# Low words of the last tile of probabilities written straight into their rows by VectorE, and the places of all heads' steps chosen anew

## The chip, the core and the metric

The kernel runs on one core of a Trainium2 chip. The core has five engines that work side by side and wait for each other by semaphores: TensorE (PE in the profile; its weight loads are PEld), VectorE (DVE), ScalarE (ACT), GpSimd (POOL), and SyncE (SP), which here only issues DMAs. Each engine runs its own instructions strictly in the order in which the program has them. The metric is the device time of one launch in microseconds. It is compared as the median of several runs.

## The reference

Attention over 8 batches of 8 heads (576 tokens, 64 columns a head) with a decay and a causal mask, then a mixer that works along the tokens and along the channels:

```python
decay = cum[:, :, :, None] - cum[:, :, None, :]
scores = np.where(causal, -1000000000.0, scale * q @ k.T + decay)
attn = np.exp(scores - max); attn = attn / (sum + 1e-09)
x = (attn @ v) laid out as [8, 576, 512]
u = x + (relu(x.T @ w_tok1) @ w_tok2).T     # w_tok1 576x256, w_tok2 256x576
out = u + relu(u @ w_ch1) @ w_ch2            # w_ch1 512x1536, w_ch2 1536x512
```

The first two lines are shortened. The weights come as float64 and are taken apart to float32 on the chip ("decoded").

## The kernel before, in words

**Precision.** PE multiplies float32 in a rounded form (fp32r in the profile). A product that must be exact is made of three: an operand is split into its high word, which is the rounded value, and its low word, which is the value minus the high word. High times high, high times low and low times high are summed in PSUM. "Low word" in what follows is always such a difference, written by a subtract (`lo_dve`, line 593, on DVE; `lo_pool`, line 590, on POOL).

**One head**, in the order of its data:
- POOL splits q and k of two heads (line 818 the high words, 826 the low ones); SP gathers them by DMA into k1 and k2 (line 873), and the decay rows into k2 (line 867).
- PE makes the scores (line 900), five tiles of rows, in PSUM. DVE adds the mask and takes the minimum (line 907, followed by a short read of the accumulator, nmin). ACT takes the exponential with the sum of each row (line 914).
- DVE makes the reciprocals (lines 932 and 935); POOL multiplies the rows by them (line 942).
- PE transposes the probabilities into PSUM (line 956) in four groups: tiles 3 and 4, tile 2, tile 1, and tile 0, which has only 64 rows of keys. For each group ACT writes the high words (line 584) and DVE the low words (line 593), into p34, p2 and p1 with both words beside each other.
- Tile 0 goes into p0, a buffer of 128 partitions: high words in partitions 0 to 63, low words in 64 to 127, so that one product with 128 rows serves both. Before the change DVE writes the low words into a buffer of their own, `low` (64 partitions, 576 columns, two subtracts of 64 and 512 columns), and POOL moves the 576 columns into the lower half of p0 (line 587). The first product with V (lines 1026 and 1027) waits for that move.
- PE multiplies with V (lines 1026 to 1038); ACT and DVE add the halves into xt (lines 1076, 1083, 1086).

Heads 0 to 3 take a short way without low words, so that the move stands in the program 60 times.

**The mixer** of a batch (transposes of xt in line 1576; the two products along the tokens in 1609 to 1612 and 1633 to 1635; the first two of twelve column blocks of the channel products in 1678 to 1680 and 1706 to 1708) is laid between the heads of the next batch, since PE would wait there. Its weights are decoded tile by tile, eight steps each on ACT, DVE and POOL (lines 682 to 702 and the split behind them), between the first 16 heads or so. The rest of the channel weights comes in 20 units of 512 columns; the first two are taken through lines 682 to 702 early, behind heads 15 to 17. After the last head the attention's buffers are given up, the other units are decoded into the space (on DVE above all), and PE makes the other ten column blocks: 768 tokens in plain form (lines 1219 to 1241), the rest with seven instead of eight products of blocks (lines 1365 to 1367 and 1440 to 1442).

**What sets the order.** The program does not write its order out. `build` gives every operation an engine, an estimated duration, a priority, and what it reads, writes and holds; `Plan.run` then plays all five engines forward, always giving a free engine the operation with the least priority number that can start by the estimates, and the sequence that comes out is the program. The priority is the head's number plus an offset of the kind of step (OFF), one of the head's place in its batch (STEP), and one of the head itself (HEAD, eight batches of eight heads). MIX, MIXB and DEC do the same for the mixer's pieces and the decode steps. In the kernel before, the HEAD and MIXB rows of batches 1 to 5 are zero: every batch there has the same places. POOL and those operations of DVE that are marked `port` are played so that one excludes the other, before the change only from batch 6 (PORT) on; earlier decode steps have longer durations instead.

Of the kernel before, what the change touches and what calls it, by code (L numbers as in the profile page):

```python
# [22 lines left out]
OFF = dict(
    load=-14.57, kh=71.94, kl=74.34, qh=-209.6, ql=-43.06, vh=-98.02, vl=123.3, s4=3.88, s3=5.49, s2=-16.37, mn=13.65,
    ex=8.87, rec=-4.02, nrm=-189.8, t3=3.09, t2=-115.31, t1=-82.69, t0=-39.76, hl=-31.61, av=-7.13, fold=-31.54,
    fpe=3.69, lo0=-44.75, fev=-192.41, u=-110.56, dec=70.59, dec2=33.11, dec3=78.27, cd=-12.6, vload=-16.33,
# [3 lines left out]
    cd=(-5.6, 64.49, 4.17, 0.29, 2.76, -5.41, -22.94, 0.01),  # L30
    kh=(17.78, -2.69, -14.75, 26.31, -2.51, -6.4, 0.84, -42.85),
    kl=(0.0, -0.21, -36.59, 1.3, -31.34, -30.51, -4.86, -5.93),
    s4=(21.98, 22.01, 19.66, -0.06, 3.68, 0.01, 62.36, 65.83),
    s3=(-5.96, 1.74, -17.12, 5.63, -13.9, 21.15, 0.16, -24.96),
    s2=(-9.31, 12.57, -3.01, -10.47, -58.87, 1.25, -0.3, -9.41),
    mn=(-20.45, -3.64, -9.81, -2.84, 19.06, -18.82, 40.74, -47.15),
    ex=(-8.49, -16.56, -25.97, 0.0, -26.61, 6.71, -17.69, 0.28),
    rec=(11.69, -16.14, -0.04, 23.14, 14.55, -4.69, 14.63, 10.44),
    nrm=(-1.09, -0.04, 34.13, -18.17, 0.0, -5.71, -23.45, -1.03),
    t3=(-47.4, -43.09, 1.3, -15.85, 0.37, -0.2, 4.51, 4.91),  # L40
    t2=(2.19, -5.45, 0.3, -22.18, 0.0, 0.51, -38.74, 2.55),
    t1=(0.03, -7.68, 5.88, 3.1, -4.1, 0.72, 10.85, 9.62),
    t0=(-29.97, 31.91, -0.46, -7.92, -108.28, -1.02, -12.55, -3.15),
    hl=(36.2, -1.08, -2.52, 2.48, 30.49, 0.0, 30.12, -19.09),
    av=(165.0, -24.98, -1.39, 1.47, -1.66, -6.57, -8.96, -9.8),
    fold=(0.54, -18.69, -70.99, 0.85, -5.32, -1.54, 57.67, -26.27),
    load=(2.05, 29.47, -1.17, -17.23, 19.8, -6.84, 2.87, 9.6),
    vload=(-5.04, 0.0, 12.21, 13.64, -0.05, 6.27, 6.41, 34.92),
    qh=(0.7, 8.11, 0.0, 0.33, 17.69, -21.0, -0.25, -0.16),
    lo0=(-2.15, 2.18, 0.0, 8.97, 0.04, -0.79, 0.22, -8.44),  # L50
# [6 lines left out]
    cd=(  # L57
# [8 lines left out]
    ),  # L66
    kh=(
# [475 lines left out]
def build(nc, env, dims):  # L543
# [20 lines left out]
    def d_act(n, ps=True, ptr=0):  # L564
        return 0.833 * n + (51 if ps else 93) + 93 * ptr + (130 if n > 512 else 0)
# [1402 lines left out]
```

## Time and profile before

| | us |
|---|---|
| median of 3 runs | 1083.37 (1082.1 to 1083.46) |
| the profiled execution | 1080.26 |
| its span | 1078.4 |
| DMA k<-hl on the chain that ended last | 6.5% of the span |
| HBM traffic over the span | 178 GB/s |

The profile shows one execution. A row of the groups view names the line of the kernel, the engine, the operation, the buffer written and those read (numbers left out), their shapes and the count; then the busy time in us, the mean of one in ns, and how long the engine idled just before these instructions, with what ended the idling. The waits view sums the same idling by who waited for whom. The windows view cuts the span into stretches. PE's clock was granted in full nearly throughout (0.995 on average). Times in rows of the timeline count from the start of the span.

### The profile page before, as it was taken

The page shows a single profiled execution, that of the slowest core. Times are in us where ns is not written, and L with a number is a line of the kernel's source. Part 1 is how long each engine was busy: PE and PEld are TensorE (multiplying, and loading weights), DVE is VectorE, ACT ScalarE, POOL GpSimd, SP SyncE. Part 2 cuts the span into 40 slices and gives each one's busy share as a digit, 9 for nine tenths or more (in the row PEclk, how much of TensorE's full clock was granted, in tenths as well). Part 3 has the DMA queues.
Part 4 walks back from the last instruction along what each step waited for, and adds up shares of the span by engine and source line. Part 5 has one row for each costly group of instructions (what it writes and reads, how often), then busy time and mean ns, then how long its engine had stood idle before and what let it go on. Part 6 is the DMA issues. An engine that isn't in the chain of part 4 may idle for free.

```text
span 1078.4 us, 20528 instructions
## 1 busy us (share of the span) xinstructions
PE 1028.6 (95%) x6442; PEld 914.1 (85%) x6442; DVE 886.8 (82%) x2117; ACT 646.8 (60%) x1607; POOL 496.8 (46%) x579
## 2 busy tenths in 40 slices
PE   8887989999999999999999899999999999999998
PEld 5566878899999999899998888877888888888887
DVE  7779989788887888878779999975995995797586
ACT  4776876788888888888777534522631541362142
POOL 4686897787868878688672100022311001102000
PEclk9999999999999999999999999999999999999999
DMA  8786785878768787686765699889899789879874
GB/s 207 187 205 144 189 211 142 205 194 201 206 174 214 198 204 204 160 221 184 216 183 188 219 328 320 260 278 346 300 304 354 237 261 342 285 218 344 247 202 148
DMA packets 143548, 248.71 MB, mean 231 GB/s; under 512 B 20760, under 2 KB 70680, under 8 KB 142416
## 3 DMA queue, kind: packets, MB, share of 16 engines
q1 hardware_dynamic: 143312, 247.39, 79.4%
q8 instruction: 52, 0.85, 0.3%
q14 instruction: 56, 0.46, 0.1%
q10 hardware_dynamic: 128, 0.01, 0.0%
HBM read 145.24 MB, written 46.66 MB: 178 GB/s over the span
## 4 chain that ended last, share of the span: by engine, by line
PE 68%; DMA 11%; DVE 10%; SPq 3%; POOL 3%; ACT 2%; issue 2%; DVEq 0%; POOLq 0%; ACTq 0%
DMA k<-hl 7%; PE bank L956 6%; PE bank L1365 5%; PE bank L1367 5%; PE bank L1366 5%; PE bank L900 4%; PE bank L1441 3%; PE bank L1440 3%; PE bank L1442 3%; PE pair L1441 2%; PE pair L1440 2%; PE pair L1442 2%; PE pair L900 2%; PE pair L1038 2%; PE pair L1036 2%
## 5 line engine op out<-in xcount | busy, mean ns | idle before, releaser
L942 POOL TENSOR_SCALAR pr<-pr,rec 128x576 f32<-128x576 f32 (+4 forms) x320 | 173.1, 561 | 37.2 <-DVE rec L935 29.5
L584 ACT ACTIVATE p<-bank 128x384 fp32r<-128x384 f32 (+2 forms) x300 | 128.1, 474 | 38.2 <-PE bank L956 36.3
L956 PE MATMUL bank<-ident,pr 128*128 128x128 f32 (+1 forms) x960 | 137.4, 276 | 7.9 <-DVE p L593 3.6
L914 ACT ACTIVATE pr<-bank,nmin 128x448 f32<-128x448 f32 (+3 forms) x256 | 118.2, 469 | 20.1 <-DVE nmin L907 17.8
L593 DVE TENSOR_TENSOR p<-bank,p 128x384 fp32r<-128x384 f32 (+1 forms) x180 | 105.9, 594 | 26.0 <-ACT p L584 25.0
L956 PEld LDWEIGHTS bank<-ident,pr 128*128 128x128 f32 (+1 forms) x960 | 107.9, 132 | 18.6 <-POOL pr L942 4.4
L907 DVE CUSTOM_DVE_ANT_0 bank<-bank,mask 64x64 f32<-64x64 f32 (+3 forms) x256 | 106.7, 432 | 14.3 <-PE bank L900 12.6
L900 PE MATMUL bank<-k 128*128 128x320 f32 (+1 forms) x496 | 87.3, 297 | 12.6 <-DMA k<-hl 7.7
L900 PEld LDWEIGHTS bank<-k 128*128 128x128 f32 x496 | 73.7, 175 | 25.7 <-DMA k<-hl 5.8
L826 POOL TENSOR_TENSOR hl<-raw,hl 128x1152 fp32r<-128x1152 f32 x28 | 74.8, 2670 | 1.4
L584 ACT ACTIVATE hid<-h 128x480 fp32r<-128x480 f32 x77 | 46.5, 605 | 48.2 <-PE bank L1441 27.0
L1038 PE MATMUL pair<-p,vv 128*128 128x512 f32 x240 | 74.0, 316 | 0.0
L1036 PE MATMUL pair<-p,vv 128*64 128x512 f32 x240 | 70.6, 335 | 0.0
L587 POOL TENSOR_SCALAR p<-low 64x576 fp32r<-64x576 f32 x60 | 42.1, 702 | 56.9 <-DVE low L593 48.5
L584 ACT ACTIVATE ring<-bank 128x288 fp32r<-128x288 f32 (+2 forms) x96 | 46.6, 496 | 20.4 <-PE bank L1576 7.3
L826 POOL TENSOR_TENSOR vv<-vr,vv 128x640 fp32r<-128x640 f32 x30 | 47.9, 1598 | 18.0 <-ACT vv L816 17.8
L593 DVE TENSOR_TENSOR low<-bank,p 64x64 fp32r<-64x64 f32 (+1 forms) x120 | 50.7, 441 | 6.6 <-ACT p L584 6.1
L1386 ACT ACTIVATE h<-bank 128x480 f32<-128x480 f32 x20 | 11.5, 573 | 73.5 <-PE bank L1367 73.5
L1377 ACT ACTIVATE tmp<-bank 128x480 f32<-128x480 f32 x20 | 11.4, 571 | 70.7 <-PE bank L1367 62.8
L590 POOL TENSOR_TENSOR ring<-xt,ring 128x576 fp32r<-128x576 f32 x32 | 45.1, 1421 | 18.5 <-ACT ring L584 17.9
L907 DVE CUSTOM_DVE_ANT_0 pair<-pair,mask 128x576 f32<-128x576 f32 x64 | 48.8, 762 | 5.8 <-PE pair L900 4.9
L584 ACT ACTIVATE st<-h 128x480 fp32r<-128x480 f32 x63 | 37.7, 604 | 25.7 <-PE bank L1441 9.4
(321 smaller groups left out, 3461.4 us busy)
## 6 DMA issues: line engine op xcount, KB each, us to landing
pw<-wd SPq DMA_DIRECT2D x280, 256.0 KB
k<-hl SPq DMA_DIRECT2D x186, 288.0 KB
raw<-in_qk SPq DMA_DIRECT2D x31, 576.0 KB
vr<-in_v SPq DMA_DIRECT2D x32, 320.0 KB
d_raw<-in_w_ch SPq DMA_DIRECT2D x80, 128.0 KB
ud<-xt SPq DMA_DIRECT2D x8, 1152.0 KB
pd<-part SPq DMA_DIRECT2D x32, 288.0 KB
wd<-pw SPq DMA_DIRECT2D x20, 384.0 KB
```

The costliest lines, as they stand in the source:

```text
L584: nc.scalar.activation(out, in_, func, scale=scale)
L593: nc.vector.tensor_tensor(out, in_, asf(hi), op=ALU.subtract)
L826: (nc.gpsimd if eng == "POOL" else nc.vector).tensor_tensor(out, in_, asf(hi), op=ALU.subtract)
L900: nc.tensor.matmul(ps[:m, of : of + w], k[:, 0, i0 : i0 + m], k[:, 1, j0 : j0 + w], start=(x == 0), stop=(fq or x == 1))
L907: nc.vector.tensor_tensor_reduce(x, x, E["mask"][:m, a : a + w], -1.0 / D**0.5, 3e38, op0=ALU.add, op1=ALU.min, accum_out=E["nmin"][sm][:m ...
L914: nc.scalar.activation(at(pr)[:m, poff[t] : poff[t] + w], at(buf)[:m, of : of + w], AF.Exp, bias=E["nmin"][sm][:m, t : t + 1], scale=-1.0, ...
L942: nc.gpsimd.tensor_scalar(x, x, r, 0.0, op0=ALU.mult, op1=ALU.add)
L956: nc.tensor.transpose(out, at(pr)[:, poff[i] + start[j] : poff[i] + end[j]], E["ident"])
L1036: nc.tensor.matmul(x[:D], at(vv)[:, v0 + j, :D], at(pb)[:, 1, c0 : c0 + w], start=False, stop=last)
L1038: nc.tensor.matmul(x, at(vv)[:, v0 + j, :], at(pb)[:, 0, c0 : c0 + w], start=False, stop=last)
L1365: nc.tensor.matmul(o, wt[:, 0, :], h_, start=(first and k == 0), stop=False, skip_group_check=True)
L1366: nc.tensor.matmul(o, wt[:, 1, :], h_, start=False, stop=False, skip_group_check=True)
```

## The change

The buffer `low` and the move on POOL are gone. DVE's two subtracts of tile 0 write their low words directly into partitions 64 to 127 of p0, while they still read PSUM and the high words in partitions 0 to 63. The first product with V waits for both of them.

```diff
-                    lambda ps=ps, w=w, pb=p0_, lb=low: lo_dve(at(lb)[:, :T0], at(ps)[:T0, w : w + T0], at(pb)[:T0, :T0]),
-                    rd=[ps, (p0_, "h0")], wr=[(low, 0)], bufs=[ps, p0_, low],
+                    lambda ps=ps, w=w, pb=p0_: lo_dve(at(pb)[T0:, :T0], at(ps)[:T0, w : w + T0], at(pb)[:T0, :T0]),
+                    rd=[ps, (p0_, "h0")], wr=[(p0_, "l0")], bufs=[ps, p0_],
...
-                "DVE", d_dve(512), n + LAG + o["t0"] + o["hl"], lambda ps=ps, pb=p0_, lb=low: lo_dve(at(lb)[:, T0:], at(ps)[:T0, :], at(pb)[:T0, T0:]),
-                rd=[ps, (p0_, "h1")], wr=[(low, 1)], bufs=[ps, p0_, low],
-            )
-
-            p.op(
-                "POOL", d_pts(S), n + LAG + o["t0"] + o["lo0"], lambda pb=p0_, lb=low: hi_pool(at(pb)[T0:, :], asf(at(lb))),
-                rd=[(low, 0), (low, 1)], wr=[(p0_, "l")], bufs=[p0_, low],
+                "DVE", d_dve(512), n + LAG + o["t0"] + o["hl"], lambda ps=ps, pb=p0_: lo_dve(at(pb)[T0:, T0:], at(ps)[:T0, :], at(pb)[:T0, T0:]),
+                rd=[ps, (p0_, "h1")], wr=[(p0_, "l1")], bufs=[ps, p0_],
```

The estimates change in a few places: POOL and the marked DVE operations now exclude each other from the start, the longer durations of the early decode steps are gone, and so is an addition for wide operations on ACT.

```diff
-        o.port = (port or eng == "POOL") and self.batch >= PORT
+        o.port = port or eng == "POOL"
...
-        return 0.833 * n + (51 if ps else 93) + 93 * ptr + (130 if n > 512 else 0)
+        return 0.833 * n + (51 if ps else 93) + 93 * ptr
...
-        p.op("DVE", d_dve(w, True) * (m2 if late else 1.8), prio, s2, wr=[gb], bufs=[gb], port=True)
+        p.op("DVE", d_dve(w, True), prio, s2, wr=[gb], bufs=[gb], port=True)
```

All the offsets are new, and the rows that were zero now hold numbers, so that every head has places of its own:

```diff
-        (0.0, 0.0, 0.0, 0.0, 0.0, 0.0, 0.0, 0.0),
+        (275.26, -91.49, 353.0, -409.24, -344.3, 66.43, 197.87, 212.99),
```

No instruction of PE, ACT, DVE or SP is added or removed. What moves is shown at three places. In these rows a name is followed by the number of its buffer (`p00_186` is p0, `low0_187` is `low`, `pr0_178` one of three buffers of probabilities), and lines from 593 on have lower numbers after the change: 593 has become 581, 907 has become 894, 942 has become 929, 1706 has become 1687.

First POOL, where heads 18 and 19 are normalised, counted from head 0. Before:

```order
L942 TENSOR_SCALAR pr0_178<-pr0_178,rec2_89 128x192
L942 TENSOR_SCALAR pr0_178<-pr0_178,rec2_89 64x64
L587 TENSOR_SCALAR p00_186<-low0_187 64x576
L942 TENSOR_SCALAR pr1_179<-pr1_179,rec3_90 128x576
L942 TENSOR_SCALAR pr1_179<-pr1_179,rec3_90 128x448
L942 TENSOR_SCALAR pr1_179<-pr1_179,rec3_90 128x320
L942 TENSOR_SCALAR pr1_179<-pr1_179,rec3_90 128x192
L942 TENSOR_SCALAR pr1_179<-pr1_179,rec3_90 64x64
L590 TENSOR_TENSOR ring3_144<-xt1_140,ring2_143 128x576
L590 TENSOR_TENSOR ring1_142<-xt1_140,ring0_141 128x576
L587 TENSOR_SCALAR p00_186<-low0_187 64x576
```

and now:

```order
L929 TENSOR_SCALAR pr1_179<-pr1_179,rec2_89 128x192
L929 TENSOR_SCALAR pr1_179<-pr1_179,rec2_89 64x64
L929 TENSOR_SCALAR pr0_178<-pr0_178,rec3_90 128x576
L929 TENSOR_SCALAR pr0_178<-pr0_178,rec3_90 128x448
L929 TENSOR_SCALAR pr0_178<-pr0_178,rec3_90 128x320
L578 TENSOR_TENSOR ring5_146<-xt1_140,ring4_145 128x576
L578 TENSOR_TENSOR ring7_148<-xt1_140,ring6_147 128x576
L929 TENSOR_SCALAR pr0_178<-pr0_178,rec3_90 128x192
L929 TENSOR_SCALAR pr0_178<-pr0_178,rec3_90 64x64
L805 TENSOR_SCALAR hl0_171<-raw0_168 128x2x576
```

The moves out of `low` are gone, and the mixer's splits (line 590, now 578) stand inside a head's normalising instead of behind it.

Next DVE, where the first two units of the later weights (in `d_g0_156` and `d_g1_157`, 512 columns) are decoded. Before, behind the minimum of head 17's widest scores:

```order
L1086 TENSOR_TENSOR xt1_140<-pair1_64,xt1_140 64x576
L690 TENSOR_SCALAR d_g0_156<-d_g0_156 128x512
L694 SCALAR_TENSOR_TENSOR d_g0_156<-d_raw2_155,d_g0_156 128x512
L932 TENSOR_SCALAR rec1_88<-sums1_84 128x3x2
L698 TENSOR_TENSOR d_g0_156<-d_g0_156 128x512
L935 RECIPROCAL rec1_88<-rec1_88 128x3x2
L702 SCALAR_TENSOR_TENSOR d_g0_156<-d_raw2_155,d_g0_156 128x512
L593 TENSOR_TENSOR p341_182<-bank4_65,p341_182 128x384
L593 TENSOR_TENSOR low0_187<-bank5_66,p00_186 64x512
L593 TENSOR_TENSOR p20_183<-bank6_67,p20_183 128x384
L593 TENSOR_TENSOR low0_187<-bank6_67,p00_186 64x64
```

and now, also behind head 17's:

```order
L581 TENSOR_TENSOR p341_182<-bank7_68,p341_182 128x384
L674 TENSOR_SCALAR d_g1_157<-d_g1_157 128x512
L674 TENSOR_SCALAR d_g0_156<-d_g0_156 128x512
L678 TENSOR_SCALAR d_g1_157<-d_g1_157 128x512
L678 TENSOR_SCALAR d_g0_156<-d_g0_156 128x512
L682 SCALAR_TENSOR_TENSOR d_g1_157<-d_raw2_155,d_g1_157 128x512
L581 TENSOR_TENSOR p00_186<-bank4_65,p00_186 64x512
L581 TENSOR_TENSOR p10_185<-bank6_67,p10_185 128x512
```

Before, the second of the two units comes to its end there. Now both begin there, side by side, and end behind heads 19 and 20. The subtract of 64x512 writes into p0 itself.

Last PE, at the mixer's product of line 1706 (now 1687) for the second batch. Before, its first pieces stand behind the 288-wide scores (`pair0_63`) of head 25:

```order
L1609 MATMUL bank6_67<-ring4_145,t1h_99 128x256
L1610 MATMUL bank6_67<-ring4_145,t1l_100 128x256
L900 MATMUL pair0_63<-k11_173 128x288
L900 MATMUL pair0_63<-k21_175 128x288
L900 MATMUL pair0_63<-k11_173 128x288
L900 MATMUL pair0_63<-k21_175 128x288
L956 MATMUL bank7_68<-ident_69,pr0_178 128x128 x3
L1706 MATMUL bank5_66<-ring8_149,w2h_105 128x288
L1707 MATMUL bank5_66<-ring8_149,w2l_106 128x288
L1708 MATMUL bank5_66<-ring9_150,w2h_105 128x288
```

and now its last pieces stand ahead of those of head 23:

```order
L1687 MATMUL bank6_67<-ring8_149,w2h_105 128x288
L1688 MATMUL bank6_67<-ring8_149,w2l_106 128x288
L1689 MATMUL bank6_67<-ring11_152,w2h_105 128x288
L1687 MATMUL bank6_67<-ring9_150,w2h_105 128x288
L1688 MATMUL bank6_67<-ring9_150,w2l_106 128x288
L1689 MATMUL bank6_67<-ring10_151,w2h_105 128x288
L887 MATMUL pair0_63<-k10_172 128x288
L887 MATMUL pair0_63<-k21_175 128x288
L887 MATMUL pair0_63<-k10_172 128x288
L887 MATMUL pair0_63<-k21_175 128x288
L887 MATMUL bank5_66<-k10_172 128x448
```

The whole product of that batch, 48 matmuls, has moved ahead of head 24.

More of the change, by code (lines that the diff above doesn't have):

```diff
@@ L27 @@
+    mn=33.01, ex=59.51, rec=-6.72, nrm=-234.7, t3=-28.78, t2=-118.02, t1=-76.37, t0=-27.57, hl=-4.25, av=-1.1,
+    fold=-10.5, fpe=5.37, fev=-216.16, u=-26.84, dec=136.36, dec2=11.47, dec3=82.64, cd=-9.19, vload=189.97,
 )
 STEP = dict(
[L30 to L50, printed above, removed]
@@ L380 @@
     START = dict(PE=3000, DVE=900, ACT=1900, POOL=1810, SP=700)
-    FIFO = ("ring", "xt", "part", "pr", "hl", "k1", "k2", "vv", "raw", "vr", "p34", "p2", "p1", "p0", "low", "hid", "hidB", "pw", "sg", "sg2", "uh", "uh2", "H", "st", "wq", "q", "rr", "g2", "d_raw", "d_g", "qf", "f34", "f2", "f1", "f0")
+    FIFO = ("ring", "xt", "part", "pr", "hl", "k1", "k2", "vv", "raw", "vr", "p34", "p2", "p1", "p0", "hid", "hidB", "pw", "sg", "sg2", "uh", "uh2", "H", "st", "wq", "q", "rr", "g2", "d_raw", "d_g", "qf", "f34", "f2", "f1", "f0")
     def __init__(self):
@@ L944, in norm @@
                 nc.vector.tensor_scalar(x, x, r, None, op0=ALU.mult)
-        p.op("DVE", 72, n + o["rec"], rec1, rd=[("sums", sm, t) for t in range(NS)], wr=[("rec", sm)])
+        p.op("DVE", 100, n + o["rec"], rec1, rd=[("sums", sm, t) for t in range(NS)], wr=[("rec", sm)])
         p.op("DVE", 100, n + o["rec"], rec2, wr=[("rec", sm)])
@@ L976, in build @@
             dur = [tp_(P, size[j]) for i, j in blocks] + ([tp_(P, T0)] if g == (2,) else [])
-            p.op("PE", dur, n + LAG + o[kind], trs, rd=[(pr, i) for i in tiles], wr=[ps], bufs=[ps, pr, pb] + (([p0_] + ([] if fv else [low])) if g == (2,) else []))
+            p.op("PE", dur, n + LAG + o[kind], trs, rd=[(pr, i) for i in tiles], wr=[ps], bufs=[ps, pr, pb] + ([p0_] if g == (2,) else []))
             if fv:
@@ L1002, in trs0 @@
                 tr(at(ps)[:T0, (i - 1) * P : i * P], i, 0)
-        p.op("PE", [tp_(P, T0)] * (NS - 1), n + LAG + o["t0"], trs0, rd=[(pr, i) for i in range(1, NS)], wr=[ps], bufs=[ps, pr, p0_] + ([] if fv else [low]))
+        p.op("PE", [tp_(P, T0)] * (NS - 1), n + LAG + o["t0"], trs0, rd=[(pr, i) for i in range(1, NS)], wr=[ps], bufs=[ps, pr, p0_])
         if fv:
@@ L1050, in build @@
         p.op(
-            "PE", d_av(512) + d_av(T0), ao, av0, rd=v_in + [(p0_, x) for x in (("h0", "h1") if fv else ("h0", "h1", "l"))],
+            "PE", d_av(512) + d_av(T0), ao, av0, rd=v_in + [(p0_, x) for x in (("h0", "h1") if fv else ("h0", "h1", "l0", "l1"))],
             wr=[(av, 0)], bufs=[av, vb, p0_, xt],
@@ L1738, in slots_of @@
     k["one"] = [(f"b{i}",) for i in (4, 5, 6, 7)]
-    for kind in ("raw", "vr", "hl", "k1", "k2", "vv", "pr", "p34", "p2", "p1", "p0", "low", "ring", "part", "xt", "d_raw", "d_g"):
+    for kind in ("raw", "vr", "hl", "k1", "k2", "vv", "pr", "p34", "p2", "p1", "p0", "ring", "part", "xt", "d_raw", "d_g"):
         k[kind] = [((kind, i),) for i in range(PRM[f"n_{kind}"])]
@@ L1862, in attn_mixer_kernel @@
         ("p0", [P, S], F32R),
-        ("low", [D, S], F32R),
     ):
```

87 lines of the change are left out of this document (50 added, 37 removed), and 374 rows, old and new, of tables (av, cd, ex, fold).

## The prediction

> **What bounds the kernel now.** First the page's busy time and the shares of the chain that ended last, then the span cut into four stages by the windows view (in each row: the stretch's length, then busy us and instruction count of PE, PEld, DVE, ACT and POOL, PE clock, DMA share, GB/s).
>
> ```profile
> PE 1028.6 (95%) x6442; PEld 914.1 (85%) x6442; DVE 886.8 (82%) x2117; ACT 646.8 (60%) x1607; POOL 496.8 (46%) x579
> PE 68%; DMA 11%; DVE 10%; SPq 3%; POOL 3%; ACT 2%; issue 2%; DVEq 0%; POOLq 0%; ACTq 0%
> 17.00:240.00 223.00, 191.75 (x1303) 162.94 (x1302) 191.15 (x535) 164.36 (x464) 171.91 (x205) 0.98 0.76 187
> 240.00:560.00 320.00, 317.18 (x2448) 302.90 (x2447) 259.46 (x769) 263.45 (x740) 248.91 (x304) 1.00 0.76 195
> 560.00:760.00 200.00, 190.01 (x1101) 166.52 (x1100) 174.97 (x375) 93.57 (x190) 29.48 (x29) 0.99 0.85 280
> 760.00:1078.00 318.00, 314.55 (x1447) 270.39 (x1445) 248.85 (x415) 119.25 (x207) 37.73 (x24) 1.00 0.84 269
> 560.00:600.00 40.00, 34.81 (x267) 32.54 (x265) 37.31 (x87) 27.73 (x64) 11.87 (x15) 1.00 0.55 186
> 600.00:640.00 40.00, 39.08 (x241) 35.91 (x242) 38.26 (x90) 20.27 (x43) 2.85 (x2) 0.96 0.89 297
> ```
>
> PE is the bound: busy 95% of the span and 68% of the last chain. Its matmuls are the same 6442 after the change, so time can only come out of PE's gaps, and the stages say where those are. From 17 to 240 us (heads 0 to 23) PE idles 223.00 - 191.75 = 31.2 us, while DVE is busy just as long as PE (191.15). From 240 to 560 us (heads 24 to 62) it idles 2.8 us: the middle is as good as full. From 560 to 760 us it idles 10.0 us, 5.2 + 0.9 of them in the first 80, where DVE, which decodes the rest of the weights there, is busy 37.31 and 38.26 of 40. From 760 us on 3.5 us are left, nearly all of them the end of the program. Busy time flatters the first stage: in the full middle a matmul costs 320 / 2448 = 0.131 us on average, by which 1303 of them are 170 us of work in 223 (an estimate, since the mixes of widths differ). So one stage has much to give, one has some, and two have nothing.
>
> Next, who PE waits for (us in total, times, longest), and the one wait on POOL that the change removes:
>
> ```profile
> PE bank L900 <- DMA k<-hl: 7.7, 13, 1.1
> PE bank L956 <- DVE p L593: 3.6, 1, 3.6
> PE bank L956 <- POOL pr L942: 1.9, 4, 0.6
> PE pair L1026 <- POOL p L587: 0.8, 1, 0.8
> POOL p L587 <- DVE low L593: 48.5, 20, 7.6
> ```
>
> **The move itself (lines 587 and 593).** The groups view has the operations that go and those that stay:
>
> ```profile
> L587 POOL TENSOR_SCALAR p<-low 64x576 fp32r<-64x576 f32 x60 | 42.1, 702 | 56.9 <-DVE low L593 48.5 <-ACT ring L584 2.1 <-DVE rec L932 1.2
> L593 DVE TENSOR_TENSOR low<-bank,p 64x512 fp32r<-64x512 f32 x60 | 40.5, 676 | 6.6 <-ACT p L584 6.1 <-POOL pr L942 0.5
> L593 DVE TENSOR_TENSOR low<-bank,p 64x64 fp32r<-64x64 f32 x60 | 12.4, 206 | 0.0
> L593 DVE TENSOR_TENSOR ring<-bank,ring 64x256 fp32r<-64x256 f32 x16 | 6.7, 418 | 0.5
> ```
>
> Removed are 60 x 702 ns = 42.1 us of POOL, one move per head from head 4 on. POOL bounds nothing by its share (46%, 3% of the chain), so these 42 us are not 42 us of time. What PE can gain from it directly is what it waited for the move (0.8) or for what stood behind a waiting move in POOL's queue: the normalised rows (1.9) and, through the splits of q and k, the gathers by DMA (7.7). That bounds this term between 0 and -10.4 us. I take -2.7, the two waits on POOL, since the gathers also wait for loads and for buffers that the change leaves alone. Late in place of the move is the DVE subtract itself, for which the first product with V now waits.
>
> That subtract now reads partitions 0 to 63 and writes 64 to 127. One kind of instruction of before does the same: the 64x256 subtract of the mixer's first rows (line 1585's, into the upper half of a ring buffer), 418 ns in the last row above. A straight line through 206 ns for 64 columns and 676 for 512 gives 206 + 470 x 192 / 448 = 407 ns for 256 (an estimate). Crossing halves thus costs some 11 ns, 60 x 2 x 0.011 = 1.3 us of DVE in all, and I take nothing for it in time.
>
> **What the change of halves costs.** The same subtract shows a second price, between instructions (the timeline; start, us, operation):
>
> ```profile
> 268.13 0.69 DVE L593 TENSOR_TENSOR p<-bank,p 128x512 fp32r<-128x512 f32 x1
> 268.86 0.42 DVE L593 TENSOR_TENSOR ring<-bank,ring 64x256 fp32r<-64x256 f32 x1
> 269.20 0.61 DVE L907 CUSTOM_DVE_ANT_0 bank<-bank,mask 128x448 f32<-128x448 f32 x1
> 269.83 0.08 DVE L907 DVE_READ_ACCUMULATOR2_ANT nmin<- 128x1 f32 x1
> 303.21 0.14 DVE L907 DVE_READ_ACCUMULATOR2_ANT nmin<- 128x1 f32 x1
> 303.38 0.42 DVE L593 TENSOR_TENSOR ring<-bank,ring 64x256 fp32r<-64x256 f32 x1
> 303.83 0.82 DVE L1083 SCALAR_TENSOR_TENSOR xt<-pair,lower,xt 128x576 f32<-128x576 f32 x1
> 304.57 0.21 DVE L907 CUSTOM_DVE_ANT_0 bank<-bank,mask 64x64 f32<-64x64 f32 x1
> ```
>
> DVE instructions mostly overlap: the one at 304.57 starts 0.08 before 303.83 + 0.82 is over, the one at 269.20 likewise. But the crossing subtract starts 0.04 and 0.03 after the end of the one ahead (268.82 and 303.35), and the next write to SBUF from partition 0 starts 0.03 and 0.02 after the end of what stands ahead of it (303.80 and 269.81). So a change of the half that DVE writes in SBUF costs about 0.03 + 0.08 = 0.11 us, where an instruction is ready behind it. In the new order these writes change halves 208 times for the low rows (into them and back), 70 of them ahead of head 24: 208 x 0.11 = 23 us of DVE, 7.7 of them in the first stage. DVE has 108 us on the chain (10% of 1078) out of 886.8 busy, so 12% of what it does sets the time: 0.12 x 23 = +2.8 us, which I take. The ends are 0, if other waits cover it all, and +23, if DVE sets the pace everywhere.
>
> The Trainium skill, page "VectorE: DVE Perf Modes", section "Two Vector instructions with no wait between them", gives this as a rule and calls it a model: an instruction whose output starts in another quadrant than the last output into the same memory is held until every earlier Vector instruction has finished. The trace agrees with it at both places. Without it the sum below would be 2.8 us less; with it in full, the first rival's time.
>
> **The order of everything else.** The new table moves work of all heads, and three counts in the two orders matter.
>
> First stage. The longest single stall there (four rows of the timeline), and three rows of the groups view, of which the first two are of the span up to 240 us:
>
> ```profile
> 93.51 5.39 POOL L942 TENSOR_SCALAR pr<-pr,rec 128x576 f32<-128x576 f32 x10
> 98.88 2.74 POOL L590 TENSOR_TENSOR ring<-xt,ring 128x576 fp32r<-128x576 f32 x2
> 97.22 4.55 DVE L690 TENSOR_SCALAR d_g<-d_g 128x256 uint32<-128x256 uint32 x1
> 102.57 1.11 PE L956 MATMUL bank<-ident,pr 128*128 128x128 f32 x4 [3.62 <-DVE p L593]
> L587 POOL TENSOR_SCALAR p<-low 64x576 fp32r<-64x576 f32 x19 | 14.2, 746 | 13.5 <-DVE low L593 9.1 <-ACT ring L584 2.1 <-DMA k<-hl 1.2
> L690 DVE TENSOR_SCALAR d_g<-d_g 128x512 uint32<-128x512 uint32 x4 | 6.1, 1528 | 0.1
> L690 DVE TENSOR_SCALAR d_g<-d_g 128x512 uint32<-128x512 uint32 x17 | 11.7, 686 | 0.1
> ```
>
> One decode step took 4.55 us, all of it beside POOL at work without a break (93.51 to 101.62), and PE idled 3.62 us behind it. The 512-wide form averages 1528 ns in the four runs before 240 us and (11.7 - 6.1) / 13 = 431 ns in the thirteen later, when POOL is nearly idle. POOL's load thus stretches these steps, and POOL now has 19 moves less in this stage, 14 us of 172. Two units of the later weights, decoded ahead in this stage, also move back on DVE, from behind heads 15 to 17 to behind heads 17 to 20. And PE gets work earlier: 1308 matmuls stand ahead of head 24's first 288-wide score in the old order, 1368 in the new, mostly the mixer's last product (line 1706) for the second batch. DVE's minimum of that score starts at 237.48 now:
>
> ```profile
> 237.48 0.79 DVE L907 CUSTOM_DVE_ANT_0 pair<-pair,mask 128x576 f32<-128x576 f32 x1
> ```
>
> If DVE and POOL bring head 24 to that point at the same time as now, 60 x 0.131 = 7.8 us of PE's work is already done. I take -7.8; the ends are 0 (the 60 are only work that PE waits behind) and -28.5 (all of the 31.2 less the 2.7 counted above).
>
> Middle. It repeats the same eight heads' places in every batch and idles 2.8 us; the new places differ from head to head. It can gain at most those 2.8, and it can lose: at the first stage's rate of idling it would be 320 x 31.2 / 223 = +45. Counted in matmuls, PE stands as far from a head's scores to its transposes in the new order as in the old, so I take +1.
>
> Transition. 3829 matmuls stand ahead of head 63's scores in the old order, 3753 in the new: 76 x 0.131 = 10 us more mixer work is left for the stretch in which PE waits for DVE's decode (6.1 us idle from 560 to 640). I take half of the idle, -3; the ends are -6.1 and +4, if the scores that now come earlier meet a later softmax.
>
> **Sum.** -2.7 + 2.8 - 7.8 + 1 - 3 = -9.7 us against the profiled execution, 1080.3 us (span 1078.4): 1070.6. The median of the runs shown, 1083.4, stands 3.1 above the profiled one. Carried over, the change gives 1073.7, and I say 1073.
>
> **Rivals.**
> The change of halves decides (15%, slower). Place: DVE from head 4 to 23, where it is busy as long as PE. Price: the whole 7.7 us, and with it the 7.8 us of early PE work is lost, since DVE brings head 24 later by as much; in the rest 12% of 15 us, +1.9. With -2.7, +1 and nothing in the transition: 1083.4 + 7.9 = 1091. It decides once DVE is busy 95% of the first stage; it now is 86%, and POOL's relief lowers it, which speaks against.
>
> The middle loses (11%, slower). A place per head instead of a repeated pattern lets small waits in: at a seventh of the first stage's rate +6.4 and more, and the gains elsewhere halved (-5): 1085 to 1095. Against it speaks that DVE, ACT and POOL idle a fifth of the middle.
>
> Hidden anyway (15%): POOL is off the path, and early PE work merely swaps one wait for another: 1080 to 1086.
>
> Nearly all early gaps go (11%): the stretched decode steps find POOL free; with two thirds of 31.2 us and the transition: 1083.4 - 21 - 6 = 1056, say 1050 to 1062.
>
> The forecast (48%): 1062 to 1080.
>
> **How the numbers follow.** About 0.2% (2.2 us) is what a measurement of this kernel can tell from no change. Faster by more: 48 + 11 + 3 of the hidden case = 62%. Within: 11% of it. Slower: 15 + 11 + 1 = 27%. The range 1056 to 1091 leaves out half of the large gain and the far ends of the two losses, about 15% together; it covers the change of halves at its full early price, while that price at every place (+23) and the far end of the middle (+45) lie beyond it, since the rows speak little for them.
>
> **What would show it.** The low-word subtracts at 676 and 206 ns as before, or longer; DVE instructions that start 0.03 after the end of the one ahead, not 0.08 before it, at those 208 places. PE's idle time in the windows: 17 to 240 us well under 31 if the early term is right, 240 to 560 near 3 if the middle holds, 560 to 640 under 6. POOL busy near 455 us. The 1528 ns of the wide decode step going down. The forecast is wrong if head 24's scores come later than 237.48 us by more than 8, or if the middle idles over 10 us.

## The result, and the profile after

| | before | after |
|---|---|---|
| median, us | 1083.41 (4 runs, 1082.1 to 1084.02) | 1100.09 (4 runs, 1096.17 to 1101.57) |
| ratio, 95% interval | 1 | 1.015 (1.0122 to 1.0178) |
| the profiled execution, us | 1080.26 | 1096.17 |
| its span, us | 1078.4 | 1094.3 |

The change makes the kernel 1.5% slower, where 1% faster was forecast; the time lies above the range. The page's busy times and chain and the windows of the stages, all of the kernel after (a window row: length, then busy us and count of PE, PEld, DVE, ACT, POOL, PE clock, DMA share, GB/s):

```profile
PE 1040.0 (95%) x6442; PEld 914.4 (84%) x6442; DVE 880.4 (80%) x2117; ACT 644.1 (59%) x1607; POOL 446.5 (41%) x519
PE 65%; DVE 13%; ACT 7%; DMA 7%; issue 3%; SPq 3%; POOL 2%; DVEq 0%; ACTq 0%; POOLq 0%
17.00:240.00 223.00, 196.67 (x1328) 164.71 (x1327) 180.21 (x519) 163.61 (x460) 147.01 (x184) 0.98 0.75 191
240.00:560.00 320.00, 308.52 (x2306) 286.18 (x2306) 260.82 (x763) 252.96 (x723) 221.27 (x262) 1.00 0.75 184
560.00:640.00 80.00, 77.15 (x545) 72.19 (x546) 69.61 (x169) 52.32 (x119) 16.77 (x20) 1.00 0.67 226
640.00:760.00 120.00, 113.32 (x608) 98.24 (x607) 98.10 (x212) 43.46 (x79) 11.04 (x11) 0.99 0.91 301
```

The longest waits of PE from 240 to 560 us (us in total, times, longest), four rows of after and then the longest row of before in the same window:

```profile
PE bank L887 <- DVE p L581: 3.0, 3, 1.3
PE bank L942 <- DVE p L581: 2.1, 4, 0.8
PE bank L942 <- ACT pr L901: 1.3, 3, 0.6
PE bank L887 <- DMA k<-hl: 0.9, 1, 0.9
```

```profile
PE bank L900 <- DMA k<-hl: 2.5, 6, 0.6
```

POOL lost its 50 us. The first stage (17 to 240 us) and the transition (560 to 640) went as forecast: PE idles 26.3 us instead of 31.2, and 2.9 instead of 6.1. But the middle (240 to 560), which was full, now idles 11.5 us instead of 2.8 and gets 2306 matmuls done instead of 2448. Most of what PE waits with there are transposes (L942) and scores (L887) whose PSUM bank DVE or ACT has not yet emptied; in before the longest wait of this window is for the gathers of k by DMA. From 640 to 760 us it idles 6.7 us instead of 3.9.

Idle time is not the whole loss. Over the span it rises from 49.8 to 54.3 us, while the busy time of the same 6442 matmuls rises from 1028.6 to 1040.0 us: they also follow one another more slowly.

**A measure by heads.** Matmuls of a stage are no fixed piece of work, so the losses were also counted by heads. The *lag* of a head is the time at which DVE takes its 128x576 minimum less the dense time of all matmuls ahead of it on PE; dense is, for each line and shape, the 30th percentile of the time from one matmul's start to the next in that trace. After minus before the lag is -8.5 us at head 21, -1.7 at head 24, +8.8 at head 39, +19.3 at head 63, and +20.0 at the end. So the early gain came, up to head 21, and from there to head 63 nearly 28 us went, 21.0 of them between heads 24 and 63. These levels hang on how dense time is taken: other ways of taking it put head 24 between -2 and -5 us, and the growth from there to head 63 at 19 to 21.

**What such a loss looks like**, in PE, then ACT, then DVE rows of the timeline (start, us, operation; in brackets the idle time ahead and what ended it):

```profile
376.76 1.15 PE L942 MATMUL bank<-ident,pr 128*128 128x128 f32 x9
378.68 0.67 PE L887 MATMUL bank<-k 128*128 128x448 f32 x2 [0.77 <-DVE p L581]
376.70 0.63 ACT L901 ACTIVATE pr<-bank,nmin 128x448 f32<-128x448 f32 x1
377.31 0.97 ACT L572 ACTIVATE p<-bank 128x512 fp32r<-128x512 f32 x2
376.44 0.79 DVE L581 TENSOR_TENSOR p<-bank,p 128x384 fp32r<-128x384 f32 x2
377.94 1.16 DVE L581 TENSOR_TENSOR p<-bank,p 128x512 fp32r<-128x512 f32 x2 [0.70 <-ACT p L572]
```

PE writes transposes into a bank, and by its order the next to use that bank are scores, with some 0.8 us of dense work between. The bank must first be read twice: by ACT's copy, which stands behind an exponential of 0.63 us, and by DVE's subtract, which waits 0.70 us for the copy. DVE ends at about 378.6, the scores start at 378.68. PE and DVE both stood idle, and neither was slow.

### The profile page after: what moved, and what is told of

Read it like the earlier page. It is cut to its first block, busy times and chain, and to the rows that moved or that the text cites. A ratio compares the mean times of both kernels' runs of the same rounds, so it can differ in the third digit from the quotient of the medians.

```text
span 1094.3 us, 20383 instructions
## 1 busy us (share of the span) xinstructions
PE 1040.0 (95%) x6442; PEld 914.4 (84%) x6442; DVE 880.4 (80%) x2117; ACT 644.1 (59%) x1607; POOL 446.5 (41%) x519
## 4 chain that ended last, share of the span: by engine, by line
PE 65%; DVE 13%; ACT 7%; DMA 7%; issue 3%; SPq 3%; POOL 2%; DVEq 0%; ACTq 0%; POOLq 0%
PE bank L1346 5%; PE bank L1347 5%; PE bank L1348 5%; PE bank L942 4%; DMA k<-hl 4%; DVE p L581 4%; ACT pr L901 3%; PE bank L887 3%; PE bank L1422 3%; PE bank L1421 3%; PE bank L1423 3%; DVE bank L894 3%; PE pair L1421 3%; PE pair L1422 3%; PE pair L1423 3%
## 5 line engine op out<-in xcount | busy, mean ns | idle before, releaser
L929 POOL TENSOR_SCALAR pr<-pr,rec 128x576 f32<-128x576 f32 (+4 forms) x320 | 164.6, 534 | 99.7 <-DVE rec L922 66.5
L581 DVE TENSOR_TENSOR p<-bank,p 128x384 fp32r<-128x384 f32 (+3 forms) x300 | 159.0, 538 | 48.3 <-ACT p L572 44.2
L942 PE MATMUL bank<-ident,pr 128*128 128x128 f32 (+1 forms) x960 | 143.0, 277 | 13.2 <-DVE p L581 8.6
L572 ACT ACTIVATE p<-bank 128x384 fp32r<-128x384 f32 (+3 forms) x300 | 130.3, 474 | 26.8 <-PE bank L942 23.4
L901 ACT ACTIVATE pr<-bank,nmin 128x320 f32<-128x320 f32 (+3 forms) x256 | 118.1, 469 | 40.7 <-DVE nmin L894 36.1
L942 PEld LDWEIGHTS bank<-ident,pr 128*128 128x128 f32 (+1 forms) x960 | 106.8, 132 | 30.8 <-DVE p L581 8.6
L894 DVE CUSTOM_DVE_ANT_0 bank<-bank,mask 128x320 f32<-128x320 f32 (+3 forms) x256 | 105.8, 435 | 12.2 <-PE bank L887 9.6
L887 PE MATMUL bank<-k 128*128 128x320 f32 (+1 forms) x496 | 85.8, 301 | 12.8 <-DVE p L581 5.4
L887 PEld LDWEIGHTS bank<-k 128*128 128x128 f32 x496 | 71.4, 175 | 25.9 <-DVE p L581 7.0
L813 POOL TENSOR_TENSOR vv<-vr,vv 128x640 fp32r<-128x640 f32 x30 | 46.9, 1562 | 34.1 <-ACT vv L803 24.5
L901 ACT ACTIVATE pr<-pair,nmin 128x576 f32<-128x576 f32 x64 | 47.3, 739 | 10.9 <-DVE nmin L894 10.6
L1449 POOL TENSOR_TENSOR d_raw<-d_raw,d_raw 128x480 f32<-128x480 f32 x11 | 15.0, 1362 | 93.0 <-DMA d_raw<-ud 68.6
L901 ACT ACTIVATION_READ_ACCUMULATOR pr<-bank,nmin 128x1 f32 (+1 forms) x256 | 51.4, 201 | 0.0
```

Of the source, the lines that this page charges most:

```text
L572: nc.scalar.activation(out, in_, func, scale=scale)
L581: nc.vector.tensor_tensor(out, in_, asf(hi), op=ALU.subtract)
L813: (nc.gpsimd if eng == "POOL" else nc.vector).tensor_tensor(out, in_, asf(hi), op=ALU.subtract)
L887: nc.tensor.matmul(ps[:m, of : of + w], k[:, 0, i0 : i0 + m], k[:, 1, j0 : j0 + w], start=(x == 0), stop=(fq or x == 1))
L894: nc.vector.tensor_tensor_reduce(x, x, E["mask"][:m, a : a + w], -1.0 / D**0.5, 3e38, op0=ALU.add, op1=ALU.min, accum_out=E["nmin"][sm][:m ...
L901: nc.scalar.activation(at(pr)[:m, poff[t] : poff[t] + w], at(buf)[:m, of : of + w], AF.Exp, bias=E["nmin"][sm][:m, t : t + 1], scale=-1.0, ...
```

## The experiments

Two things were changed together, how the low words reach their rows and the order of everything. Every run below keeps one order word for word, unless it says otherwise. PE's idle time in the middle is 320 less the busy time of the window from 240 to 560 us. The diffs show only the calls that change, shortened, and of several alike only one: of tile 0's two subtracts the one of 512 columns.

| kernel | order | low words of tile 0 | ratio to before, 95% interval | PE idle, 240 to 560 | matmuls there |
|---|---|---|---|---|---|
| before | old | buffer, GpSimd move | 1 | 2.8 | 2448 |
| e10 | old | neither move nor holds | 0.9988 (0.9956 to 1.002) | 1.6 | 2460 |
| e1 | old | direct | 1.0061 (1.0029 to 1.0092) | 1.8 | 2430 |
| e3 | old | upper buffer, move | 1.0068 (1.0036 to 1.01) | 1.6 | 2428 |
| e9 | new | neither move nor holds | 1.0107 (1.0049 to 1.0164) | 11.7 | 2331 |
| after | new | direct | 1.015 (1.0122 to 1.0178) | 11.5 | 2306 |
| e4 | new | direct, halves exchanged | 1.021 (1.017 to 1.025) | 14.1 | 2267 |
| e2 | new | buffer, GpSimd move | 1.0256 (1.0215 to 1.0298) | 20.4 | 2245 |

### The old order with the direct write (e1)

```diff
-lo_dve(at(lb)[:, T0:], at(ps)[:T0, :], at(pb)[:T0, T0:])
+lo_dve(at(pb)[T0:, T0:], at(ps)[:T0, :], at(pb)[:T0, T0:])
...
-lambda pb=p0_, lb=low: hi_pool(at(pb)[T0:, :], asf(at(lb)))
+lambda: None
```

> The order of the kernel before, word for word on PE, ACT and SP, with only the direct write: the two subtracts write partitions 64 to 127 of the rows, and GpSimd's move is not issued. Theory H (the middle stage lost because VectorE now changes halves, some 0.11 us each time, 208 times): the middle, 240 to 560 us, idles 8 to 12 us of PE instead of 2.8, and the time is 1090 to 1100. Theory O (the middle lost because of the new order alone): the middle idles about 3 us, and the time is 1080 to 1084, less what the 60 moves cost on GpSimd (0 to 3 us).

Measured: 1090.52 us (10 runs; before 1081.85 in 19 of the same session), ratio 1.0061, and 1.8 us of idle time in the middle:

```profile
240.00:560.00 320.00, 318.22 (x2430) 300.30 (x2429) 265.24 (x774) 262.09 (x737) 221.37 (x263) 1.00 0.75 192
```

Each theory is half right: the time rises as H said, but not in the middle. Where it rises this profile doesn't show, since its first stage ran at a lower clock (0.93 against 0.98 in before).

### The new order with the move (e2)

```diff
+(lo_dve(E["low"][:, T0:], at(ps)[:T0, :], at(pb)[:T0, T0:]),
+ hi_pool(at(pb)[T0:, :], asf(E["low"])))
```

> The order of the kernel after, word for word on PE, ACT, SP, and on VectorE too except that the two subtracts write the low buffer in partitions 0 to 63 again; GpSimd moves it into the rows at once behind the second subtract, 60 more instructions of 0.7 us on its queue. Theory H: no change of halves, so the middle idles 3 to 4 us, the gains ahead of head 24 and in the transition stay, and the time is 1070 to 1078. Theory O: the middle still idles 10 us or more, and the time is 1097 to 1106.

Measured: 1111.21 us, ratio 1.0256. The middle is lost although no half changes, which speaks against theory H; the time that theory O gave is missed too. The moves cost much here: e9 (below) has the same order with neither moves nor holds, and its ratio is 1.5% lower. The new order was made without a place for them on POOL, and the largest wait of PE from 240 to 560 us is for such a move:

```profile
PE pair L1007 <- POOL p L575: 5.2, 6, 2.4
```

So this run alone doesn't tell the order from the moves; e9 does.

### The old order with the change of halves alone (e3)

```diff
-("low", [D, S], F32R)
+("low", [P, S], F32R)
...
-lo_dve(at(lb)[:, T0:], at(ps)...
+lo_dve(at(lb)[T0:, T0:], at(ps)...
...
-hi_pool(at(pb)[T0:, :], asf(at(lb)))
+hi_pool(at(pb)[T0:, :], asf(at(lb)[T0:]))
```

> The kernel before with the low buffer in partitions 64 to 127 instead of 0 to 63: its order and GpSimd's move are kept, only the halves that VectorE writes change. Theory H: as the old order with the direct write, plus the moves: 1090 to 1102, with the middle idle 8 to 12 us. Theory O: 1083 to 1086, each change costing VectorE 0.1 us that its slack takes up.

Measured: 1088.79 us, ratio 1.0068: the price of e1 with the move still there. So within the intervals (some 3.5 us to each side) the whole of e1's loss is the holds, and taking the move away beside them brings nothing.

### The new order with the halves exchanged (e4)

```diff
-hi_act(at(pb)[:T0, T0:], at(ps)[:T0, :])
+hi_act(at(pb)[T0:, T0:], at(ps)[:T0, :])
-lo_dve(at(pb)[T0:, T0:], at(ps)[:T0, :], at(pb)[:T0, T0:])
+lo_dve(at(pb)[:T0, T0:], at(ps)[:T0, :], at(pb)[T0:, T0:])
```

> The kernel after with the halves of the row tile exchanged: ScalarE writes the rounded words into partitions 64 to 127, VectorE the low words into 0 to 63 (V's rows stand twice in its tile, so the product is the same sum). VectorE changes no half of what it writes; it reads the other half of SBUF. Theory H: the middle idles 3 to 4 us, the time is 1070 to 1077. Theory O: 1097 to 1101, as after. If reading the other half holds VectorE as writing it does: 1097 to 1101 too, with 31 ns instead of an overlap of 76 ns ahead of the subtracts.

Measured: 1106.57 us, ratio 1.021, slower even than after and above the 1097 to 1101 of every case that kept the loss. The mechanism of the third case is there all the same: reading the other half of SBUF holds VectorE too. Why it costs more than in after is not shown; starts held in this way are no more frequent (280 against 292, counted as explained below). The same three instructions in the kernel after, in e4, and in e9 (below), which stays in one half:

```profile
308.97 0.82 DVE L1064 SCALAR_TENSOR_TENSOR xt<-pair,lower,xt 128x576 f32<-128x576 f32 x1 [0.17 <-ACT xt L1057]
309.82 0.68 DVE L581 TENSOR_TENSOR p<-bank,p 64x512 fp32r<-64x512 f32 x1
310.43 0.41 DVE L581 TENSOR_TENSOR ring<-bank,ring 64x256 fp32r<-64x256 f32 x1
```

```profile
313.50 0.82 DVE L1064 SCALAR_TENSOR_TENSOR xt<-pair,lower,xt 128x576 f32<-128x576 f32 x1 [0.18 <-ACT xt L1057]
314.35 0.68 DVE L581 TENSOR_TENSOR p<-bank,p 64x512 fp32r<-64x512 f32 x1
315.06 0.42 DVE L581 TENSOR_TENSOR ring<-bank,ring 64x256 fp32r<-64x256 f32 x1
```

```profile
314.50 0.82 DVE L1064 SCALAR_TENSOR_TENSOR xt<-pair,lower,xt 128x576 f32<-128x576 f32 x1 [0.19 <-ACT xt L1057]
315.23 0.67 DVE L581 TENSOR_TENSOR p<-bank,p 64x512 fp32r<-64x512 f32 x1
315.93 0.42 DVE L581 TENSOR_TENSOR ring<-bank,ring 64x256 fp32r<-64x256 f32 x1
```

Only in e9 does the 64x512 subtract start ahead of the end of what stands before it (315.23 against 315.32). In after it is held because it writes the upper half (309.82 against 309.79), in e4 because it reads it (314.35 against 314.32).

### Parts of the new places (e5 to e8)

The new offsets, with the planner's durations that belong to them, for some batches only, the old ones for the rest, always with the direct write. The planner then makes the order anew.

```diff
+NEWB = (0, 1, 2)        # e6: (3, 4, 5)   e7: (6, 7, 8)   e8: (0, 1, 2, 6, 7, 8)
+new = b in NEWB
+oo, ss, hh = (OFF_A, STEP_A, HEAD_A) if new else (OFF, STEP, HEAD)
 o = {k: oo[k] + x[h] + hh[k][b % 8][h] for k, x in ss.items()}
```

> Direct write; places, planner's prices and the decode's places of the change for the heads and the mixer of batches 0 to 2 alone, those of before from head 24 on. The lag of a head is the time at which VectorE takes its first 128x576 scores less the dense time of the matmuls ahead of it on PE; against before it was -8.5 us at head 21 and +19.3 at head 63 in the kernel after, +10.3 and +12.8 in the old order with the direct write. Theory P (what is lost sits in the places of the middle, batches 3 to 5): lag -8 at head 21 and -4 to -6 at head 63, time 1074 to 1080. Rival R (the new first stage only runs ahead by leaving work for the middle, which pays it back): lag at head 63 +6 or more, time 1086 to 1096.

> Direct write; places and prices of the change for batches 3 to 5 alone. Theory P: lag +10 at head 21 as in the old order, and 18 to 25 us more by head 54, time 1104 to 1114. Rival R: the middle loses no more than 3 us, as in the old order with the direct write, time 1088 to 1093.

> Direct write; places and prices of the change from batch 6 on alone, the transition's decode with them. Both theories: lag +10 at head 21 and +12 at head 48; from there on a gain of 0 to 4 us in the transition against the old order with the direct write, time 1085 to 1091; a loss of 4 us or more between heads 48 and 63 would put part of the middle's loss into batch 6.

> Direct write; places and prices of the change for batches 0 to 2 and from batch 6 on, those of before for batches 3 to 5 alone. Theory P: as with the new places in batches 0 to 2 alone, with a transition better by 0 to 3: 1071 to 1079, faster than both kernels. Rival R: 1084 to 1094.

Measured: 1147.55, 1136.14, 1110.33 and 1140.86 us, ratios 1.0596, 1.0502, 1.0248 and 1.0533; PE idle in the middle 34.1, 32.6, 10.9 and 30.3 us. No theory expected anything like it. From head 24 on e5 has the old places, which leave PE 1.8 us idle in e1, and here 34.1. A likely reason, which no run shows, is what the offsets are: they pick among what can start, so what they yield hangs on the state that the heads before leave. The runs tell that the places are no sum of parts; they don't tell which part is at fault, and theory P and rival R stay undecided by them.

### Neither move nor holds, in both orders (e9, e10)

```diff
-lo_dve(at(pb)[T0:, T0:], at(ps)[:T0, :], at(pb)[:T0, T0:])
+lo_dve(at(pb)[:T0, T0:], at(ps)[:T0, :], at(pb)[:T0, T0:])
```

> The order of the kernel after, word for word, with neither the move nor a change of halves: the two subtracts write over the rounded words in partitions 0 to 63, and partitions 64 to 127 of the rows hold zeros throughout, so one of the two products of the first 64 keys is left out. Theory O (the new order loses the middle by itself): from head 24 to head 63 the lag still grows by 15 to 21 us (21.0 in the kernel after), and the time is 1089 to 1097, the kernel after less what the holds cost. Theory B (it loses it only together with the holds or with the moves): the lag grows by 8 at most, 1074 to 1084.

> The order of the kernel before, word for word, with neither the move nor a change of halves, the same product left out. What the 60 moves cost GpSimd's neighbours, alone. If nothing (GpSimd is idle half of the time): 1079 to 1084, as before, and lag +0 to -1 at head 63. If the first stage pays for them: 1071 to 1078, lag -4 or lower at head 21. Against it, the old order with the direct write gives the price of the holds.

Measured: e9 1094.87 us, ratio 1.0107; e10 1081.13 us, ratio 0.9988 (before 1081.17 beside both). The first window row is e9's, the second e10's:

```profile
240.00:560.00 320.00, 308.28 (x2331) 287.68 (x2329) 256.24 (x769) 253.85 (x724) 222.27 (x264) 1.00 0.75 186
```

```profile
240.00:560.00 320.00, 318.44 (x2460) 303.97 (x2459) 262.19 (x784) 263.85 (x740) 225.84 (x268) 1.00 0.76 196
```

This takes the change apart. The order alone costs 1.0107 - 0.9988 = 1.2%, 12.9 us (e9's interval is 6 us to each side), and the loss shows in the middle. The lag grows by 17.7 us more than before's between heads 24 and 63 in e9 (theory O), and shrinks by 1.3 in e10. The direct write's holds cost 1.0061 - 0.9988 = 0.73%, 7.9 us, in the old order, where the two intervals don't meet. In the new order the difference is 1.015 - 1.0107 = 0.43%, 4.7 us, but there the intervals overlap, so that this price is not told from nothing. With POOL's 42 us of moves gone in the old order the time changed by -1.3 us in e10, where the interval, -4.8 to +2.2 us, holds no change.

### The same instructions of heads 24 to 63 in other places (e11)

```diff
 order = p.run(slots_of())
+order = [order[i] for i in PLACE]
```

> The kernel after with its instructions of heads 24 to 63 put in other places on PE, VectorE, ScalarE and GpSimd, by exchanging neighbours where it shortens the planner's own schedule; nothing is added or taken out, and the first stage and what follows head 63 keep their order. Theory O: the lag grows by 7 to 14 instead of 21 between heads 24 and 63, and the time is 1085 to 1094. If the middle's loss lies in the holds or in contention and not in the places: 1097 to 1102.

Measured: 1092.01 us (10 runs), ratio 1.0085 (1.0053 to 1.0117), against 1.015 for the kernel after. The lag grows by 16.0 instead of 21.0 us, less of a change than expected, and PE idles 8.2 us in the middle. With the same instructions, holds and all, other places give back some 7 us by the ratios, 8 by the medians: the time that theory O gave was met, its lag of 7 to 14 was not. What PE waits for in e11's middle is mostly the gathers of k by DMA (5.5 us, against 0.9 in after).

### The same over the whole program, old order (e12, e13)

> The old order with the direct write, its instructions put in other places in the same way over the whole program, with 0.107 us more for each of the two subtracts. If places in the queues found by such exchanges hold on the chip: 1066 to 1080, faster than both kernels. If they don't carry: 1086 to 1094, as the old order with the direct write or worse.

> The kernel before, low buffer and GpSimd's move kept, its instructions put in other places over the whole program by exchanging neighbours where it shortens the planner's own schedule. In the old order with the direct write the same gave back 8 us. If that was the places and not the direct write: 1072 to 1077, faster than both kernels. If it only hid the holds, which are not in this kernel: 1080 to 1084.

Measured: e12 1082.56 us, ratio 1.0019 (0.9986 to 1.0051), which is no longer told from before, while its interval still overlaps e1's; e13 1086.84 us (12 runs), ratio 1.0052 (1.0029 to 1.0074), slower than before. Both miss. The exchanges were made where the planner's own durations come out shorter, and as far as e11 to e13 show, they agree with the chip where an order loses much and don't carry to the order of before. No kernel tried here is faster than before.

### One engine's work cut in the middle (f1 to f4)

From head 24 on; the diff is f1's, f2 cuts `hi_act` in the same way, f3 the normalising, f4 is f1 and f2 together.

```diff
-lambda ps=ps, pb=pb, w=w: lo_dve(at(pb)[:, 1, :], at(ps)[:, :w], at(pb)[:, 0, :])
+lambda ps=ps, pb=pb, w=w // (1 + (n >= 24)): lo_dve(at(pb)[:, 1, :w], at(ps)[:, :w], at(pb)[:, 0, :w])
```

> The kernel after, every instruction in its place, but from head 24 on VectorE's five subtracts of low words of the transposed probabilities cover only half of their columns (half of these low words are left out): some 1 us of VectorE less in each of 40 heads, 39 us in all. If PE waits in the middle because VectorE as a whole is too slow: the lag grows by 5 at most between heads 24 and 63 (21.0 in the kernel after), and the time is 1078 to 1085. If PE waits at the banks behind a chain of two engines, copy on ScalarE and then subtract on VectorE, of which only one link is shortened: 13 to 17, and 1091 to 1097.

> The kernel after, every instruction in its place, but from head 24 on ScalarE's five copies of the rounded words of the transposed probabilities cover only half of their columns (the other half keeps what stood there): some 0.8 us of ScalarE less in each head. If ScalarE as a whole is too slow: the lag grows by 5 at most, 1078 to 1085. If it is one link of the chain that empties the banks: 13 to 18, and 1091 to 1097. If ScalarE doesn't matter: 20 to 22, and 1098 to 1102.

> The kernel after, every instruction in its place, but from head 24 on GpSimd normalises only half of the columns of each tile of probabilities (the rest stays as the exponents left it): some 0.7 us of GpSimd less in each head. If PE's transposes wait for GpSimd in the middle: the lag grows by 12 at most, 1085 to 1093. If GpSimd is off the path there: 19 to 22, and 1098 to 1102.

> The kernel after, every instruction in its place, with both cuts from head 24 on: the copies on ScalarE and the subtracts on VectorE cover half of the columns of the transposed probabilities. If the two together are what PE waits for, since each alone gave back 5 to 6 us: the lag of heads 24 to 63 grows by 6 to 12 against before, 1083 to 1089. If PE waits for the places of these instructions in their queues (behind others that wait themselves), and not for their length: it grows by 14 or more, 1089 to 1095.

| | cut | median, us | ratio, 95% interval | lag of heads 24 to 63, more than before's | PE idle, 240 to 560 |
|---|---|---|---|---|---|
| after | none | 1100.09 | 1.015 (1.0122 to 1.0178) | 21.0 | 11.5 |
| f1 | DVE | 1093.65 | 1.0118 (1.0083 to 1.0152) | 21.7 | 13.1 |
| f2 | ACT | 1092.8 | 1.0109 (1.0081 to 1.0136) | 16.0 | 11.4 |
| f3 | POOL | 1098.24 | 1.0155 (1.0126 to 1.0184) | 19.3 | 10.4 |
| f4 | DVE and ACT | 1091.62 | 1.01 (1.0032 to 1.0169) | 17.0 | 11.7 |

```profile
240.00:560.00 320.00, 308.34 (x2340) 290.18 (x2340) 232.23 (x769) 230.50 (x725) 222.04 (x264) 0.99 0.75 187
```

The row is f4's. DVE is 29 us less busy in the middle than after, ACT 22, and PE idles as long as before the cuts. POOL is off the path (f3). A cut of either link gives 6.4 and 7.3 us in the medians, but 3.5 and 4.4 by the ratios, each against before in its own session, and the intervals overlap that of after; the one profiled execution of f1 doesn't show a gain in the middle, so where these come from stays open. Both cuts together give 5.4 by the ratios. Time and lag came as expected for a link of a chain in f2, for POOL off the path in f3 and for places in the queues in f4; in f1 the time did, the lag (13 to 17) not. Shorter instructions thus win back about a third of what after loses. What PE waits for changes, though: in f4's middle the two longest waits are for the gathers of k by DMA, 4.9 us in all where after has 0.9.

```profile
PE bank L887 <- DMA k<-hl: 3.1, 4, 1.0
PE pair L887 <- DMA k<-hl: 1.8, 2, 0.9
```

So with ACT and DVE sooner at the banks, other waits stand in the place of theirs. Whether the new order's late gathers cost time of their own was not tried; no run moves them alone.

## Why the prediction was wrong, point by point

**The move, -2.7: measured -1.3, not told from nothing.** e10 against before is 0.9988, and its interval, -4.8 to +2.2 us, holds 0 as well as -2.7; the far end of the term, -10.4, is out. The prediction took it that both waits on POOL vanish with the move. The one for the normalised rows, 1.9 us, doesn't: in e10 PE waits 2.7 us for them over the span:

```profile
PE bank L956 <- POOL pr L942: 2.7, 5, 1.0
```

**The change of halves, +2.8: right in kind, measured 1.7 and 2.8 times as large.** The predicted signature is there at the predicted places: counting DVE instructions that start 8 to 45 ns behind the end of the one ahead, up to 650 us, the direct write has 292 in the new order where e9 has 121, and 295 in the old where e10 has 134. That is some 160 to 170 holds for the 208 forecast, at 0.107 us about 18 us of DVE. They cost 4.7 us (not told from nothing) and 7.9 us, which is 26% and 44% of that. The share of DVE on the chain, 12%, was the step that failed: it is an average over the program. A likely reason that the holds cost more is that they stand beside ACT's copies in the chain that frees PSUM; no run shows it. The 11 ns for crossing halves came: the two subtracts took 682 and 218 ns instead of 676 and 206.

**The first stage, -7.8: it came, and most of it went again ahead of head 24.** The lag was -8.5 us at head 21 at the same clock (0.98) as before. At head 24 it was -1.7, by other ways of taking dense time up to -5; its minimum started at 241.08 us, 3.6 later than before, within the 8 that was named. By the prediction's own price the 60 matmuls less 3.6 us would leave 4.2 of the 7.8. The stretched decode step fell as said:

```profile
L678 DVE TENSOR_SCALAR d_g<-d_g 128x512 uint32<-128x512 uint32 x4 | 1.5, 407 | 0.0
```

It was 1528 ns. So the condition of the term, that DVE and POOL bring head 24 to its scores at the same time as now, failed by 3.6 us, though the 60 matmuls did stand ahead of it.

**The middle, +1: this is the step that failed.** It cost 21 us of lag, and PE idles 11.5 us, over the 10 at which the text called itself wrong. The prediction took +1 because "PE stands as far from a head's scores to its transposes in the new order as in the old". That distance did not shrink. Others did: those from the transposes in a single PSUM bank to the next matmuls in the same bank. To the next scores, in heads 24 to 47 and in dense time of the matmuls between, the median went from 2.59 to 2.02 us and the shortest tenth from 1.68 to 1.19 (21 cases in before, 25 in after). With the next transposes counted in, less than 1.3 us stood between in none of 88 cases in heads 24 to 62 of before, and in 8 of 103 of after. The time lost ahead of matmuls that are the first to enter such a bank was 6.0 us in heads 24 to 62 before and 20.6 after; 4.2 in e10 and 17.3 in e9, 12.5 in e11, 13.2 in f4. That is 14.6 of the 21.6 us that all matmuls of these heads lost more (28.4 before, 50.0 after). Short distances are only part of it: of the 13.8 us that were lost more ahead of such matmuls from 240 to 560 us, the waits with under 1.3 us between two transposes, or transposes and scores, make 5.4; in the others ACT or DVE comes to the bank late for want of something else, as in the rows shown above. That a bank is entered too soon is thus measured as the place of the loss; which part of the order brings it about stays open.

The rival "the middle loses" named the place, with "a place per head instead of a repeated pattern" as its mechanism, and priced it at +6.4. Shown is that the order does it, without holds or moves (e9), and that other places for the same instructions lessen it (e11). That the lack of a repeated pattern is what makes it worse was not tried alone, and stays argued: mixing the tables (e5 to e8) upset everything else with it.

**The transition, -3: right in its window only.** From 560 to 640 us 6.1 us of idle time became 2.9. From 640 to 760 us 2.8 came back, and the lag, +19.3 us at head 63 and +20.0 at the end, shows no gain behind head 63.

**The sum.** By the ratios e10's -1.3, the order's 12.9 and the holds' 4.7 make 16.3 us. As differences between the same runs they must add up to after less before, so this is no test of them. In the prediction the order stood for -9.8 and the holds for +2.8.

## What to carry to other kernels

A stage without idle time has only one way to go when its order is made anew: look there first, and compare for each shared buffer, PSUM banks above all, how much of PE's work lies between one user and the next, not only how far a result is from its use. An engine's share of the chain that ended last is an average over the program and can price a small cost on that engine too low: here 12% was taken, and 44% was measured in the old order. To take a change of order and code apart, run the new code in the old order and the old order without the cost: here e1 against e10 priced the write, and e9 against e10 the order.

## What the runs showed of the hardware

VectorE is held by what it reads as by what it writes: in e4 the 64x512 subtract writes the same half as the one ahead of it and reads the other, and starts 0.03 us behind its end (314.35 against 314.32). The minima that follow such a subtract read SBUF from partition 0 again and write PSUM: in e4 they start 31 ns behind its end in the median, in after 76 ns ahead of it. The Trainium skill, page "VectorE: DVE Perf Modes", section "Two Vector instructions with no wait between them", has this in its model: the start quadrant of an input is compared with that of the last input read from the same memory, as the output's is with the last output. The trace agrees.

The clock that PE was granted differed between executions of the same work: from 17 to 240 us it was 0.98 in the profiled executions of before and after, 0.95 in those of e9 and e10, 0.93 in that of e1. A difference of 0.05 is some 10 us of the 190 that PE is busy there, more than most effects studied here. Over more than a hundred executions on record, an execution of the same kernel whose mean granted clock is 0.01 lower takes some 8 us longer (a straight line through them). Allowing for that changes no conclusion above: after is then +16.3 us against before, e9 +12.5, e1 +6.0, e3 +6.4, e10 -1.2, e11 +10.4. Lags in the first stage were therefore compared only at equal clocks, and times by the ratios of several runs.
